# Exponentials on VectorE in an attention kernel: three SBUF passes for five, and groups that may open nearer to a unit's end

## The chip, the cores and the metric

The kernel runs on one core of one Trainium2 chip. The metric is the device time of one execution in microseconds (us). Each kernel was run in several rounds beside the kernel before on the same chip. One of the runs of the kernel before (993.6 us, in the series of e5 to e8) was slow and is not used. A ratio within 2% of 1 counts as "the same" in the record; where an interval below lies clear of 1, the difference is still called faster or slower here.

The engines are called as in the profile: PE is TensorE (matmul), ACT is ScalarE, DVE is VectorE, POOL is GpSimd, SP issues DMAs. In a profile, L1253 is a line of the kernel's source. The changed kernel is one to four lines shorter, so the same operation has a slightly lower line number there.

## The reference

One transformer block on 2,048 tokens of width 512: layer norm, attention with 32 heads of 16, residual, layer norm, a gated FFN of width 1,792, residual. What matters here is the softmax:

```python
scores = jnp.einsum("bhqd,bhkd->bhqk", q, k) * (Dh ** -0.5)   # 32 x 2048 x 2048
p = _softmax(scores, axis=-1)
o = jnp.einsum("bhqk,bhkd->bhqd", p, v)
```

That is 134 million exponentials. The kernel takes them as 2,048 tiles of 128 keys by 512 queries (for the last two query chunks: two key blocks by 256 queries).

## The kernel before

The program is not written down in its final order. A builder in Python holds streams of operations, each with an estimated duration, and emits them greedily: whatever can start first on an engine, by priority. Its order is then fixed, engine by engine. Work goes in 40 units (a query chunk and four heads): 24 of 64 tiles and 16 of 32.

Most tiles are exponentiated by ACT straight from PSUM, in steps of three and two tiles that use five PSUM banks in turn. A score step therefore waits for the exp two steps before it:

```python
SLOTS = ((0, 3), (3, 2))                       # PSUM banks of the two alternating steps
NRING = 15                                      # places of the ring PT that holds ACT's results
def exps():
    ...
    yield Op("act", 0.093 + 0.427 * n, ACTF(PT[:, p0:p0 + n, :], pbank[:, b0:b0 + n, :], ACT.Exp, scale=LN2 / 1024, bias=...))
```

An exp writes into PT, a ring of 15 tiles. It also has to wait until the PV matmul (the product with V) of the tile that was in its place before is done.

Some tiles go to DVE, in groups of up to four. A group takes four PSUM banks one after the other from the two that the dense work (projections, FFN) also uses. Each tile is converted to a 16-bit integer on its way from PSUM to SBUF, then the group is processed as a whole. The exponential comes out as a sum of two tiles, and PE sums them: it streams both against V.

```python
def dconv(G, j, b):                             # one per tile
    yield Op("dve", 0.7, ... tensor_scalar(out=dX[...], in0=pbank[:, b, :], scalar1=XMIN + 1024.0 * CENTER, scalar2=XMIN, op0=ALU.add, op1=ALU.max))
def dchain(G):                                  # once per group, five passes
    W = X & 0x3ff | 0x3c00                      # tensor_scalar
    W = W * W                                   # tensor_tensor
    W = -EK * ESCALE * W - ESCALE               # tensor_scalar
    E = (X >> 3) & 0x1f80                       # tensor_scalar
    X = W * X                                   # tensor_tensor
def pv():                                       # the group's part of it
    fns += prod(i, [dE2[:, d, j, :], dX[:, x, j, :].bitcast(BF16)])   # two PV streams per tile
```

(The passes are shortened here to what they compute.) Three rules decide when a group may open; there are three group buffers (`NX = 3`):

```python
GLAST = 32; DGAP = 6.0; DBUSY = 2.0; LOOK = 0.12; RATE = 1250
def room():        # no fourth group before the first one's PV; DVE not far behind; DGAP us since the last opening, ...
    ... C["gk"] - C["gpv"] >= NX ... sch.now >= C["dnext"] + (DBUSY if C["down"] < first_t[C["cdone"]] else 0)
def over(G):       # a group takes no more tiles once GLAST or fewer tiles of its unit are left
    return bool(G["t"]) and unit0[G["u"] + 1] - C["qpos"] <= GLAST
def pick(G):       # with fewer than GLAST + 12 tiles left, a new group is for the next unit
    u = unit_of(nxt) + (pos_of(nxt)[1] - pos_of(nxt)[0] < GLAST + 12)
```

Where PE would fall behind a rate of 1,250 columns per us the builder adds filler matmuls of zeros (`zero_bf` against `ones_bf`). At the end the kernel checks that all softmax sums lie in a range and runs a slower path if not.

## Time and profile before

The median of three runs was 913.09 us (912.94 to 913.13).

| what | view | before |
|---|---|---|
| PE, DVE, ACT busy | engine shares | 853.2, 738.0, 849.1 us of 909.8 |
| exp steps of ACT | groups by shape | 356 of three tiles, 356 of two: 1,780 tiles |
| tiles of DVE | conversions in the groups | 268, in 72 groups |
| ACT waiting for PE's attention matmuls | list of waits | 21.4 us, 36 waits |
| fillers | groups | 392, 133.7 us |

The page of the kernel before, engine shares:

```profile
PE 853.2 (94%) x7245; PEld 278.8 (31%) x7245; DVE 738.0 (81%) x1138; ACT 849.1 (93%) x782; POOL 210.6 (23%) x247
```

Its groups with shapes kept apart; after the count stand busy us, mean ns of one instruction, then the engine's idle time before them:

```profile
L1253 ACT ACTIVATE PT<-pbank 128x1536 bf16<-128x1536 f32 x356 | 533.3, 1498 | 21.4 <-PE pbank L1247 20.0
L1253 ACT ACTIVATE PT<-pbank 128x1024 bf16<-128x1024 f32 x356 | 383.5, 1077 | 1.5 <-PE pbank L1247 1.4
...
L1566 DVE TENSOR_SCALAR dX<-pbank 128x512 uint16<-128x512 f32 x268 | 181.5, 687 | 60.8 <-PE pbank L1247 58.7
L1582 DVE TENSOR_TENSOR dW<-dW 128x2048 f16<-128x2048 f16 x59 | 73.6, 1248 | 0.9
L1587 DVE TENSOR_TENSOR dX<-dW,dX 128x2048 bf16<-128x2048 bf16 x59 | 73.6, 1247 | 0.9
L1584 DVE TENSOR_SCALAR dE<-dX 128x2048 uint16<-128x2048 uint16 x59 | 44.7, 758 | 0.0
L1583 DVE TENSOR_SCALAR dW<-dW 128x2048 bf16<-128x2048 f16 x59 | 42.3, 717 | 0.7
...
L1581 DVE TENSOR_SCALAR dW<-dX 128x2048 uint16<-128x2048 uint16 x59 | 40.4, 685 | 0.4
```

ACT is the engine that is nearly always busy with the work that the softmax is made of. The two tensor_tensor passes of a full group take 1,248 and 1,247 ns, the tensor_scalar passes 685 to 758 ns.

The list of waits of ACT, its first line (us in total, times, longest):

```profile
ACT PT L1253 <- PE pbank L1247: 21.4, 36, 3.5
```

By the matmul whose semaphore came last before each exp in the trace, 17.1 us are for scores and 4.3 for PV.

Two stretches, one without FFN work and one with it (POOL is only used by the FFN there):

```profile
150.00:225.00 75.00, 67.77 (x525) 18.87 (x521) 69.08 (x96) 72.60 (x65) 0.00 (x0) 1.00 0.01 1
260.00:345.00 85.00, 80.78 (x553) 22.34 (x553) 71.12 (x98) 84.33 (x82) 48.45 (x40) 1.00 0.00 1
```

In the first, DVE is busy 69.1 of 75 us.

### The profile page before, as it was taken

To read this page: it belongs to the slowest core of one execution; us is meant where nothing else is said; L and a number is where in the kernel's file an instruction comes from. 1 tells how busy PE (TensorE), PEld (TensorE's weight loads), DVE (VectorE), ACT (ScalarE), POOL (GpSimd) and SP (SyncE) were. 2 spreads that over 40 slices of the span, in tenths; PEclk is the share of its full clock that TensorE was granted. 3 is DMA by queue.
4 is the path that set the end of the run, shared out by engine and by line. 5 is a ranking of instruction groups with operands and counts; after the bars stand their busy time and mean duration, and the time that the engine had idled before them with its cause. 6 is when DMAs were issued, how large, how long until landed. Compare 5 with 4: busy or idle time off the path is not lost.

```text
span 909.8 us, 17576 instructions
## 1 busy us (share of the span) xinstructions
PE 853.2 (94%) x7245; PEld 278.8 (31%) x7245; DVE 738.0 (81%) x1138; ACT 849.1 (93%) x782; POOL 210.6 (23%) x247
## 2 busy tenths in 40 slices
PE   8999999998999999999899999999999999999987
PEld 3322222222232222222232222222233333333435
DVE  7668899999888889799968888899977877876752
ACT  4699999999999999999999999999999999999951
POOL 5600000000034752000025743000004354340500
PEclk9999999999999999999999999999999999999999
DMA  5000061000000000000000000000000000001000
GB/s 186 1 1 1 1 223 34 1 1 2 12 1 1 1 2 1 18 18 2 1 12 1 2 1 7 13 18 1 1 14 13 2 1 1 2 7 30 1 13 16
DMA packets 12330, 15.11 MB, mean 17 GB/s; under 512 B 1744, under 2 KB 11216, under 8 KB 12240
## 3 DMA queue, kind: packets, MB, share of 16 engines
q1 hardware_dynamic: 12240, 13.90, 4.7%
q8 instruction: 58, 0.95, 0.4%
q14 instruction: 32, 0.26, 0.1%
HBM read 11.80 MB, written 2.10 MB: 15 GB/s over the span
## 4 chain that ended last, share of the span: by engine, by line
PE 50%; ACT 30%; issue 12%; DVE 6%; DMA 1%; SPq 0%; POOL 0%; ACTq 0%; DVEq 0%
ACT PT L1253 29%; PE pbank L1247 26%; PE pbank L1246 17%; PE pbank L1847 4%; PE pbank L1250 1%; ACT w_sb L1775 1%; DVE w_sb L1776 1%; DVE dX L1566 1%; DMA wqkv_sb<-in_A_wqkv_dram 1%; DVE OA L1653 1%; DVE dW L1582 1%; DVE dE L1584 0%; DVE QT L1391 0%; DVE g_sb L1765 0%; DVE dW L1581 0%
## 5 line engine op out<-in xcount | busy, mean ns | idle before, releaser
L1253 ACT ACTIVATE PT<-pbank 128x1536 bf16<-128x1536 f32 x712 | 819.5, 1288 | 22.9 <-PE pbank L1247 21.4
L1247 PE MATMUL pbank<-QT,KT 32*128 32x512 bf16 (+1 forms) x2560 | 313.0, 340 | 36.5 <-ACT PT L1253 28.9
L1566 DVE TENSOR_SCALAR dX<-pbank 128x512 uint16<-128x512 f32 x268 | 181.5, 687 | 60.8 <-PE pbank L1247 58.7
L1247 PE MATMUL pbank<-PT,VA 128*17 128x512 bf16 (+1 forms) x2235 | 180.0, 339 | 0.0
L1247 PEld LDWEIGHTS pbank<-QT,KT 32*128 32x128 bf16 x2560 | 82.8, 91 | 297.9 <-ACT PT L1253 207.6
L1847 PE MATMUL pbank<-ones_bf,zero_bf 128*128 128x512 bf16 x392 | 133.7, 386 | 6.4 <-DVE OA L1653 6.4
L1718 POOL TENSOR_SCALAR rstd<-mv 128x1 f32<-128x1 f32 x16 | 3.6, 226 | 483.2 <-DVE mv L1716 483.2
L1767 POOL TENSOR_TENSOR w_sb<-g_sb 128x512 f32<-128x512 f32 x49 | 65.1, 1330 | 167.8 <-DVE g_sb L1765 167.3
L1582 DVE TENSOR_TENSOR dW<-dW 128x2048 f16<-128x2048 f16 (+3 forms) x72 | 86.7, 1204 | 1.1
L1587 DVE TENSOR_TENSOR dX<-dW,dX 128x2048 bf16<-128x2048 bf16 (+3 forms) x72 | 85.2, 1184 | 1.1
L1247 PEld LDWEIGHTS pbank<-PT,VA 128*17 128x17 bf16 x2235 | 46.1, 87 | 107.4 <-issue 102.0
L1769 POOL TENSOR_TENSOR w_sb<-w_sb,g_sb 128x512 f32<-128x512 f32 x49 | 69.7, 1432 | 3.0
L1246 PE MATMUL pbank<-hnT_c,wg_sb 128*128 128x512 bf16 (+1 forms) x280 | 63.6, 339 | 1.0 <-ACT hnT_c L1692 0.5
L1246 PE MATMUL pbank<-hnT_c,wu_sb 128*128 128x512 bf16 (+1 forms) x280 | 62.8, 339 | 0.5 <-DVE dX L1566 0.4
L1246 PE MATMUL pbank<-wd_sb,GUT 128*128 128x512 bf16 x224 | 59.2, 382 | 0.0
L1584 DVE TENSOR_SCALAR dE<-dX 128x2048 uint16<-128x2048 uint16 (+3 forms) x72 | 52.6, 731 | 0.0
L1847 PEld LDWEIGHTS pbank<-ones_bf,zero_bf 128*128 128x128 bf16 x392 | 31.4, 96 | 68.3 <-issue 56.3
L1583 DVE TENSOR_SCALAR dW<-dW 128x2048 bf16<-128x2048 f16 (+3 forms) x72 | 50.1, 695 | 0.8
L1581 DVE TENSOR_SCALAR dW<-dX 128x2048 uint16<-128x2048 uint16 (+3 forms) x72 | 48.1, 668 | 0.4
L1776 DVE SCALAR_TENSOR_TENSOR w_sb<-w_sb,g_sb 128x512 f32<-128x512 f32 x49 | 40.6, 832 | 8.1 <-ACT w_sb L1775 7.7
L1799 DVE SCALAR_TENSOR_TENSOR GUT<-pbank,w_sb 128x512 bf16<-128x512 f32 x49 | 33.4, 687 | 14.8 <-PE pbank L1246 14.5
L1765 DVE COPY g_sb<-pbank 128x512 f32<-128x512 f32 x49 | 33.5, 685 | 10.7 <-PE pbank L1246 10.4
(89 smaller groups left out, 613.0 us busy)
## 6 DMA issues: line engine op xcount, KB each, us to landing
xres<-in_A_x_dram SPq DMA_DIRECT2D x16, 128.0 KB, 2.2
out_dram<-out_sb SPq DMA_DIRECT2D x16, 128.0 KB, 1.7
wg_sb<-in_B_w_gate_dram SPq DMA_DIRECT2D x1, 1792.0 KB, 7.1
wu_sb<-in_B_w_up_dram SPq DMA_DIRECT2D x1, 1792.0 KB, 11.9
wd_sb<-in_B_w_down_dram SPq DMA_DIRECT2D x1, 1792.0 KB, 17.3
x_sb<-in_A_x_dram SPq DMA_DIRECT2D x3, 512.0 KB, 8.6
wqkv_sb<-in_A_wqkv_dram SPq DMA_DIRECT2D x1, 896.0 KB, 7.7
x_sb<-in_A_x_dram SPq DMA_DIRECT2D x2, 256.0 KB, 2.9
```

The costliest lines, as they stand in the source:

```text
L1246: return lambda e: e.matmul(o, l, r, start=start, stop=stop)
L1247: return lambda e: e.matmul(o, l, r, start=start, stop=stop, tile_position=tile)
L1253: return lambda e: e.activation(out=o, in_=i, func=func, **kw)
L1566: yield Op("dve", 0.7, lambda e: e.tensor_scalar(out=dX[:, G["k"] % NX, j, :], in0=pbank[:, b, :], scalar1=XMIN + 1024.0 * CENTER, scalar2 ...
L1582: yield Op("dve", t2, lambda e: e.tensor_tensor(out=W, in0=W, in1=W, op=ALU.mult), reads=kW, writes=kW, port=True)
L1583: yield Op("dve", t1, lambda e: e.tensor_scalar(out=WB, in0=W, scalar1=-EK * ESCALE, scalar2=-ESCALE, op0=ALU.mult, op1=ALU.add), reads=kW ...
L1584: yield Op("dve", t1, lambda e: e.tensor_scalar(out=E.bitcast(U16), in0=X, scalar1=3, scalar2=0x1f80, op0=ALU.logical_shift_right, op1=ALU ...
L1587: yield Op("dve", t2, lambda e: e.tensor_tensor(out=X.bitcast(BF16), in0=WB, in1=X.bitcast(F16), op=ALU.mult), reads=kW + kX, writes=kX, p ...
L1767: yield Op("pool", 1.13, lambda e: e.tensor_tensor(out=ws, in0=gs, in1=gs, op=ALU.mult), reads=[("g", i)], writes=[("w", i)])
L1769: yield Op("pool", 1.3, lambda e: e.tensor_tensor(out=ws, in0=ws, in1=gs, op=ALU.mult), reads=[("w", i), ("g", i)], writes=[("w", i)])
L1776: yield Op("dve", 0.68, lambda e: e.scalar_tensor_tensor(out=ws, in0=ws, scalar=1.0, in1=gs, op0=ALU.add, op1=ALU.mult), reads=[("w", i), ...
L1847: fill_op = Op("pe", TMM, lambda e: e.matmul(pbank[:, PVB, :], zero_bf[:], ones_bf[:], start=False, stop=False, skip_group_check=True), re ...
```

## The change

The intent: with another split of the exponential, 2^n(1 + 2m/3 + m*m/3) up to a constant, three passes over a group are enough, and DVE's tiles stay fp16. DVE should then take more tiles from ACT. So that it can, a group takes tiles until 16 of the unit are left instead of 32 (the cut-off), a new one opens for a unit with at least 28 left instead of 44, and 3 us after the last instead of 6 (the gap).

```diff
-GLAST = 32
+GLAST = 16
-DGAP = 6.0
+DGAP = 3.0
-    dE2 = at("dE2", [128, NE, GS, 512], BF16)
+    dE2 = at("dE2", [128, NE, GS, 512], F16)
... (the exp's bias, the ones column of V, the V evacuation and the range check follow the new constants)
 def dchain(G):
-  ... tensor_scalar(out=W.bitcast(U16), in0=X, scalar1=0x3ff, scalar2=0x3c00, op0=ALU.bitwise_and, op1=ALU.bitwise_or)
-  ... tensor_tensor(out=W, in0=W, in1=W, op=ALU.mult)
-  ... tensor_scalar(out=WB, in0=W, scalar1=-EK * ESCALE, scalar2=-ESCALE, op0=ALU.mult, op1=ALU.add)
-  ... tensor_scalar(out=E.bitcast(U16), in0=X, scalar1=3, scalar2=0x1f80, op0=ALU.logical_shift_right, op1=ALU.bitwise_and)
+  ... tensor_scalar(out=W.bitcast(U16), in0=X, scalar1=0x3ff, scalar2=0xb800, op0=ALU.bitwise_and, op1=ALU.bitwise_or)
+  ... tensor_scalar(out=E.bitcast(U16), in0=X, scalar1=0x7c00, scalar2=0x8, op0=ALU.bitwise_and, op1=ALU.bitwise_or)
-  ... tensor_tensor(out=X.bitcast(BF16), in0=WB, in1=X.bitcast(F16), op=ALU.mult)
+  ... tensor_tensor(out=X.bitcast(F16), in0=W, in1=X.bitcast(F16), op=ALU.mult)
 def pv():
-  fns += prod(i, [dE2[:, d, j, :], dX[:, x, j, :].bitcast(BF16)])
+  fns += prod(i, [dE2[:, d, j, :], dX[:, x, j, :].bitcast(F16)])
```

More of the change, by code (lines that the diff above doesn't have):

```diff
@@ L1094 @@
 CENTER = 12
-EC, EK = 0.46167356, 0.16665046
-ESCALE = 2.0 ** -80
-VSCALE = 2.0 ** (95 - CENTER)
+EFIT = 1.5068958
+PSCALE = EFIT * 2.0 ** (CENTER - 15)
 def bass_sequential_preLN__mha_block__geglu_ffn__prompt_kernel(nc, A_x, A_wqkv, A_wo, B_x, B_w_gate, B_w_up, B_w_down, out):
@@ L1284, in consts @@
         yield Op("pool", 0.3, lambda e: e.tensor_copy(out=ident32[:], in_=ident[:]), reads=["ident"], writes=["ident32"])
-        yield Op("pool", 2.3, lambda e: e.memset(VA[:, :, :, 16:17], VSCALE), writes=["VA_ones"])
+        yield Op("pool", 2.3, lambda e: e.memset(VA[:, :, :, 16:17], 1.0), writes=["VA_ones"])
     def masks():
@@ L1402, in proj_v @@
                                       for dc in (2 * hf, 2 * hf + 1)], reads=rd, writes=[("pb", b)])
-            op = Op("dve", 0.61, lambda e, b=b, t=t: e.tensor_scalar(out=VA[:, t, :, 0:16], in0=pbank[:, b, :].rearrange("p (h i) -> p h i", i=16), scalar1=VSCALE, scalar2=None, op0=ALU.mult),
+            op = Op("dve", 0.61, lambda e, b=b, t=t: e.tensor_copy(out=VA[:, t, :, 0:16], in_=pbank[:, b, :].rearrange("p (h i) -> p h i", i=16)),
                     reads=[("pb", b)], writes=[("V", t)])
@@ L1490, in exps @@
             p0, n = an % NRING, len(mine)
-            yield Op("act", 0.093 + 0.427 * n, ACTF(PT[:, p0:p0 + n, :], pbank[:, b0:b0 + n, :], ACT.Exp, scale=LN2 / 1024, bias=-LN2 * (95 - CENTER) - math.log(EC)),
+            yield Op("act", 0.093 + 0.427 * n, ACTF(PT[:, p0:p0 + n, :], pbank[:, b0:b0 + n, :], ACT.Exp, scale=LN2 / 1024, bias=math.log(PSCALE)),
                      reads=[("pb", b0 + k) for k in range(n)], writes=[("PT", p0 + k) for k in range(n)],
@@ L1576, in dchain @@
         X, W, E = dX[:, x, 0:n, :], dW[:, 0:n, :], dE2[:, d, 0:n, :]
-        WB = W.bitcast(BF16)
         kX, kW, kE = [("dX", x, j) for j in range(n)], ["dW"], [("dE", d)]
@@ L1580, in dchain @@
         yield Wait(lambda: G["conv"] == n)
-        yield Op("dve", t1, lambda e: e.tensor_scalar(out=W.bitcast(U16), in0=X, scalar1=0x3ff, scalar2=0x3c00, op0=ALU.bitwise_and, op1=ALU.bitwise_or), reads=kX, writes=kW, port=True)
-        yield Op("dve", t2, lambda e: e.tensor_tensor(out=W, in0=W, in1=W, op=ALU.mult), reads=kW, writes=kW, port=True)
-        yield Op("dve", t1, lambda e: e.tensor_scalar(out=WB, in0=W, scalar1=-EK * ESCALE, scalar2=-ESCALE, op0=ALU.mult, op1=ALU.add), reads=kW, writes=kW, port=True)
-        yield Op("dve", t1, lambda e: e.tensor_scalar(out=E.bitcast(U16), in0=X, scalar1=3, scalar2=0x1f80, op0=ALU.logical_shift_right, op1=ALU.bitwise_and), reads=kX, writes=kE, port=True,
+        yield Op("dve", t1, lambda e: e.tensor_scalar(out=W.bitcast(U16), in0=X, scalar1=0x3ff, scalar2=0xb800, op0=ALU.bitwise_and, op1=ALU.bitwise_or), reads=kX, writes=kW, port=True)
+        yield Op("dve", t1, lambda e: e.tensor_scalar(out=E.bitcast(U16), in0=X, scalar1=0x7c00, scalar2=0x8, op0=ALU.bitwise_and, op1=ALU.bitwise_or), reads=kX, writes=kE, port=True,
                  gate=lambda: C["gpv"] >= G["k"] - NE + 1)
         C["gw"] += 1
-        yield Op("dve", t2, lambda e: e.tensor_tensor(out=X.bitcast(BF16), in0=WB, in1=X.bitcast(F16), op=ALU.mult), reads=kW + kX, writes=kX, port=True)
+        yield Op("dve", t2, lambda e: e.tensor_tensor(out=X.bitcast(F16), in0=W, in1=X.bitcast(F16), op=ALU.mult), reads=kW + kX, writes=kX, port=True)
         G["done"] = 1
@@ L1831, in check @@
         yield Op("dve", 0.1, lambda e: e.tensor_scalar(out=LCHK[:, n:n + 1], in0=probe[:, 0:1], scalar1=65535.0, scalar2=None, op0=ALU.is_equal), reads=["probe"] + [("LINV", u) for u in range(NU)], writes=["probe", "LCHK"])
-        yield Op("dve", 0.4, lambda e: e.tensor_scalar(out=LCHK[:, 0:n], in0=lf, scalar1=2.0 ** -40, scalar2=2.0 ** -10, op0=ALU.max, op1=ALU.min),
+        yield Op("dve", 0.4, lambda e: e.tensor_scalar(out=LCHK[:, 0:n], in0=lf, scalar1=2.0 ** -40, scalar2=2.0 ** -6, op0=ALU.max, op1=ALU.min),
                  reads=[("LINV", u) for u in range(NU)], writes=["LCHK"])
```

## The prediction

> **What bounds it now.** ScalarE. The table of engine shares gives ACT 849 of 909.8 us (93%). The group list gives its exps as 356 steps of three 512-column tiles at 1,498 ns and 356 of two at 1,077 ns: 0.515 us a tile. The list of waits gives ACT only 21.4 us of waiting for score matmuls. Exps run from 16 to 875 us; about 35 us of tail follow.
>
> Of 2,048 tiles, 268 go to VectorE, in 72 groups (59 are full). A full group costs it four conversions, about 2.5 us back to back (each recorded as 0.69, started 0.61 apart), and five passes: 0.69 + 1.25 + 0.72 + 0.76 + 1.25 = 4.66 us as recorded, about 4.5 back to back. Together 7.0 us. Where no FFN work runs (150 to 225 us) VectorE is busy 69.1 of 75 us and a group comes every 8 us: VectorE limits what it can take over. In FFN stretches (260 to 345 us) it takes only 12 to 14 tiles per 50 us against 26; VectorE is 84% busy there, TensorE 95%.
>
> **What the change removes, adds, moves.** Two passes go: the square (86.7 us in all) and the scale-and-offset (50.1 us). The three that stay keep shapes and widths, so durations should stay: about 0.69, 0.76, 1.25 us. The Trainium skill, "VectorE: DVE Perf Modes", section "What auto-detection actually checks", says that a two-tensor operation reaches only the two-per-cycle mode, a one-source one from SBUF four per cycle; the trace agrees (1.25 against 0.69 to 0.76 us): one expensive and one cheap pass go. A group then costs about 5.1 us, 27% less. The exp's bias, the ones column and the V evacuation cost the same. fp16 tiles against bf16 weights: no change expected, though no run here shows it yet.
>
> The smaller gap and the later cut-off let the freed time be used. Each tile moved saves ACT 0.515 us and costs TensorE about one more PV stream, an estimated 0.1 us; TensorE has 134 us of filler matmuls to give up, mostly outside FFN stretches.
>
> **How much is on the path.** Outside FFN work (about 375 us): tiles per 50 us go from 26 to 32 or 33 on top of ACT's 110, some 5%, 19 us. FFN stretches between 250 and 560 us: about 3.5%, 7 us. After 650 us, with small query chunks, few fillers and a nearly full TensorE: 1.5%, 3 us. Head and tail keep their length. Sum 29 us: 913 to 884 us. That is about 325 VectorE tiles in 85 to 90 groups, ACT exps near 888 us (summed durations) against 917, VectorE busy 690 us instead of 738, fillers down from 392 to about 300.
>
> **Chances.** 884 us, range 866 to 899. Faster by over 2% (under 894.8): 0.82; within 2%: 0.16; slower: 0.02.
>
> **What would show each step.** Three passes per group at unchanged durations; over 300 conversions; about 690 ACT exp steps instead of 712; groups every 6 us or less where no FFN runs. ACT should stay over 92% busy there; if its waits for score matmuls pass 45 us, TensorE or the PV order has become the limit.
>
> **What would make it wrong.** Groups limited by something other than VectorE time (two shared PSUM banks, three group buffers, the next unit's scores): tiles stay near 280, VectorE idles, time near 905. Late groups delaying a unit's last PV, so that ACT runs out of ring slots. TensorE filling up. On the other side, if VectorE stays 92% busy everywhere, 350 tiles and about 868 us. A failed range check would run the fallback and double the time.

## The result

The changed kernel takes 904.62 us (median of 4 runs, 901.49 to 905.76) beside 913.11 us before. Ratios are the mean time of one kernel's fast runs over that of the other's of the same rounds, so not quite the ratio of the medians: 0.9899, with a 95% interval of 0.988 to 0.9918. That is 1% faster, within the 2% that counts as the same. The range of 866 to 899 us does not hold it.

The same views of the changed kernel. Engine shares, groups by shape, the waits of ACT, the two stretches:

```profile
PE 852.3 (94%) x7220; PEld 277.2 (31%) x7220; DVE 682.1 (75%) x1093; ACT 827.7 (92%) x761; POOL 202.1 (22%) x247
```

```profile
L1252 ACT ACTIVATE PT<-pbank 128x1536 bf16<-128x1536 f32 x345 | 510.1, 1479 | 34.4 <-PE pbank L1246 32.8
L1252 ACT ACTIVATE PT<-pbank 128x1024 bf16<-128x1024 f32 x345 | 364.0, 1055 | 2.0 <-PE pbank L1246 1.8
...
L1565 DVE TENSOR_SCALAR dX<-pbank 128x512 uint16<-128x512 f32 x322 | 216.8, 686 | 86.4 <-PE pbank L1246 84.4
L1583 DVE TENSOR_TENSOR dX<-dW,dX 128x2048 f16<-128x2048 f16 x69 | 87.0, 1261 | 0.9
L1580 DVE TENSOR_SCALAR dE<-dX 128x2048 uint16<-128x2048 uint16 x69 | 51.7, 749 | 0.0
L1579 DVE TENSOR_SCALAR dW<-dX 128x2048 uint16<-128x2048 uint16 x69 | 50.7, 735 | 0.5
```

```profile
ACT PT L1252 <- PE pbank L1246: 34.6, 53, 3.5
```

```profile
150.00:225.00 75.00, 70.99 (x552) 19.87 (x551) 66.50 (x101) 74.13 (x66) 0.00 (x0) 1.00 0.01 1
260.00:345.00 85.00, 80.11 (x575) 22.04 (x574) 68.83 (x102) 83.67 (x80) 42.69 (x39) 1.00 0.00 1
```

Nearly everything that was forecast about the work is there: three passes at about their old durations (735 ns against 685 in the first, the others within 2%), 322 tiles (forecast 325) in 87 groups, 691 exp steps with the one odd one (690), DVE busy 682 us (690), 303 fillers (about 300). ACT is busy 21.4 us less (849.1 to 827.7). But the span fell by only 5.8 us in the profiled runs (909.8 to 904.0). So the time in which ACT does nothing grew from 60.7 to 76.3 us, by 15.6 us, and 13.2 us of that are waits for PE's attention matmuls (21.4 to 34.6): 10.3 us more for scores (17.1 to 27.4) and 2.9 us more for PV (4.3 to 7.2). The question is why ACT waits more.

The four runs differ by the granted clock: 901.49 us at 1.000, then 904.08 at 0.996, 905.16 at 0.994 and 905.76 us at 0.993. The trace's clock records show three stretches of 3.4 us at half speed in the profiled run and one that begins 2.7 us before its end; in the kernel before there is only one, 0.2 us before the end. By the four runs (905.76 less 901.49 us) that is worth some 4 us of the gap, not 20.

### The profile page after: what moved, and what is told of

It reads as the page before. It is cut to its first block, busy times and chain, and to the rows that moved or that the text cites. A ratio compares the mean times of both kernels' runs of the same rounds, so it can differ in the third digit from the quotient of the medians.

```text
span 904.0 us, 17467 instructions
## 1 busy us (share of the span) xinstructions
PE 852.3 (94%) x7220; PEld 277.2 (31%) x7220; DVE 682.1 (75%) x1093; ACT 827.7 (92%) x761; POOL 202.1 (22%) x247
## 4 chain that ended last, share of the span: by engine, by line
PE 57%; ACT 20%; DVE 11%; issue 10%; POOL 1%; ACTq 0%; DVEq 0%; POOLq 0%
PE pbank L1246 31%; ACT PT L1252 20%; PE pbank L1245 17%; PE pbank L1843 5%; DVE dX L1565 3%; PE pbank L1249 1%; DVE w_sb L1772 1%; DVE OA L1649 1%; DVE dE L1580 1%; PE pbank L1840 1%; DVE dX L1583 1%; DVE g_sb L1761 1%; ACT w_sb L1771 1%; DVE dW L1579 1%; PE pbank L1853 0%
## 5 line engine op out<-in xcount | busy, mean ns | idle before, releaser
L1252 ACT ACTIVATE PT<-pbank 128x1536 bf16<-128x1536 f32 (+1 forms) x691 | 796.7, 1266 | 36.5 <-PE pbank L1246 34.6
L1246 PE MATMUL pbank<-QT,KT 32*128 32x512 bf16 (+1 forms) x2560 | 320.6, 340 | 22.2 <-ACT PT L1252 17.0
L1565 DVE TENSOR_SCALAR dX<-pbank 128x512 uint16<-128x512 f32 x322 | 216.8, 686 | 86.4 <-PE pbank L1246 84.4
L1843 PE MATMUL pbank<-ones_bf,zero_bf 128*128 128x512 bf16 x303 | 105.4, 388 | 11.3 <-DVE OA L1649 11.3
L1583 DVE TENSOR_TENSOR dX<-dW,dX 128x2048 f16<-128x2048 f16 (+3 forms) x87 | 103.1, 1185 | 1.3
L1763 POOL TENSOR_TENSOR w_sb<-g_sb 128x512 f32<-128x512 f32 x49 | 55.7, 1137 | 163.0 <-DVE g_sb L1761 162.6
L1580 DVE TENSOR_SCALAR dE<-dX 128x2048 uint16<-128x2048 uint16 (+3 forms) x87 | 63.1, 725 | 0.0
L1579 DVE TENSOR_SCALAR dW<-dX 128x2048 uint16<-128x2048 uint16 (+3 forms) x87 | 60.6, 697 | 0.7
L1246 PE MATMUL pbank<-dE,VA 128*17 128x512 f16 (+1 forms) x385 | 38.0, 347 | 0.0
L1246 PE MATMUL pbank<-dX,VA 128*17 128x512 f16 (+1 forms) x385 | 37.6, 344 | 0.0
## 6 DMA issues: line engine op xcount, KB each, us to landing
wd_sb<-in_B_w_down_dram SPq DMA_DIRECT2D x1, 1792.0 KB, 16.6
```

The costliest lines, as they stand in the source:

```text
L1246: return lambda e: e.matmul(o, l, r, start=start, stop=stop, tile_position=tile)
L1252: return lambda e: e.activation(out=o, in_=i, func=func, **kw)
L1565: yield Op("dve", 0.7, lambda e: e.tensor_scalar(out=dX[:, G["k"] % NX, j, :], in0=pbank[:, b, :], scalar1=XMIN + 1024.0 * CENTER, scalar2 ...
L1579: yield Op("dve", t1, lambda e: e.tensor_scalar(out=W.bitcast(U16), in0=X, scalar1=0x3ff, scalar2=0xb800, op0=ALU.bitwise_and, op1=ALU.bit ...
L1580: yield Op("dve", t1, lambda e: e.tensor_scalar(out=E.bitcast(U16), in0=X, scalar1=0x7c00, scalar2=0x8, op0=ALU.bitwise_and, op1=ALU.bitwi ...
L1583: yield Op("dve", t2, lambda e: e.tensor_tensor(out=X.bitcast(F16), in0=W, in1=X.bitcast(F16), op=ALU.mult), reads=kW + kX, writes=kX, por ...
```

## The experiments

All kernels give the right result (e9 only by its slower path, see there). "Waits" are ACT's waits for scores and PV together, from the list of waits of the profiled run; "PV" is the part of them that a PV matmul ended, worked out from the trace's semaphores. "Tiles" are those of DVE. "Clock" is that of the profiled run.

| kernel | passes | cut-off | tiles | ACT busy, us | waits, us | PV, us | clock | median, us |
|---|---|---|---|---|---|---|---|---|
| before | 5 | 32 | 268 | 849.1 | 21.4 | 4.3 | 1.000 | 913.11 |
| after | 3 | 16 | 322 | 827.7 | 34.6 | 7.2 | 0.993 | 904.62 |
| e1 passes only | 3 | 32 | 293 | 840.1 | 44.1 | 17.1 | 0.992 | 923.34 |
| e2 passes and cut-off | 3 | 16 | 308 | 833.0 | 28.6 | 6.3 | 0.993 | 905.50 |
| e3 cut-off alone | 5 | 16 | 261 | 853.7 | 31.9 | 11.5 | 0.996 | 934.01 |
| e4 sum on DVE | 3+1 | 16 | 282 | 844.0 | 25.1 | 3.6 | 0.993 | 912.12 |
| e5 few fillers | 3 | 16 | 321 | 832.7 | 57.7 | 7.7 | 0.883 | 934.87 |
| e6 few fillers, before | 5 | 32 | 270 | 855.1 | 68.1 | 12.8 | 0.857 | 969.74 |
| e7 more fillers | 3 | 16 | 325 | 834.0 | 77.3 | 38.8 | 0.998 | 955.33 |
| e8 cut-off 18 | 3 | 18 | 308 | 832.9 | 29.9 | 11.7 | 0.998 | 907.81 |
| e9 look-ahead 0.10, before | 5 | 32 | 268 | | 41.6 | 16.6 | | (fallback) |
| e10 look-ahead 0.10, after | 3 | 16 | 324 | 827.0 | 38.8 | 12.5 | 0.995 | 908.51 |
| e11 PV sets apart | 3 | 32 | 284 | 842.0 | 25.1 | 4.4 | 0.998 | 911.39 |
| e12 other constants | 3 | 16 | 326 | 824.4 | 23.4 | 2.9 | 0.997 | 890.56 |
| e13 new numbers, old order | 5 | 32 | 268 | 849.3 | 23.8 | 5.7 | 0.995 | 913.06 |
| e14 look-ahead 0.14, before | 5 | 32 | 265 | 853.1 | 37.0 | 7.4 | 0.984 | 929.56 |
| e15 look-ahead 0.14, after | 3 | 16 | 322 | 826.8 | 36.9 | 6.8 | 0.987 | 912.26 |
| e16 constants of e12, before | 5 | 32 | 262 | 854.2 | 32.7 | 12.3 | 0.996 | 934.49 |

ACT's busy time follows the tiles within some 3 us, but for e5 to e7, where it is 5 to 10 us higher than in kernels with about as many tiles (a likely reason: exps overlap in the records only where ACT does not wait, and these three wait most). The waits do not follow the tiles, and they are what moves the time about.

### e1, e2, e3: the parts of the change

```diff
e1  -GLAST = 16    +GLAST = 32      -DGAP = 3.0   +DGAP = 6.0      (from the changed kernel)
e2  -DGAP = 3.0    +DGAP = 6.0                                     (from the changed kernel)
e3  -GLAST = 32    +GLAST = 16                                     (from the kernel before)
```

> Three passes, with the old gap (6) and the old cut-off (32); its program moves 293 tiles to VectorE instead of 268 (after: 322). Theory T1 (TensorE is what the moved tiles run into: each costs it nearly what ScalarE saves): the gain is small and roughly in step with the tiles, so 906 to 911 us. Rival T2 (the later cut-off hurts: groups that open late hold up the last PV of a unit and eat a larger gain of the passes): this is at least as fast as the whole change, 904 us or less, with fewer waits of TensorE for VectorE.

> Three passes and the new cut-off (16), old gap (6): 308 tiles. T1: between e1 and the whole change, 903 to 908 us. T2: as slow as the whole change or slower, while e1 is faster. If the gap is what hurts, this is clearly faster than the whole change (under 900).

> The kernel before, five passes, with only the cut-off at 16; the smaller gap makes no difference to that program. 261 tiles, seven fewer than before. T1: the same as before or up to 5 us slower (910 to 918). T2: clearly slower than before (over 920), since the slower chains hold up the units' ends more.

Measured: e1 923.34 us, ratio 1.0101 (1.0082 to 1.0121). The three passes alone, with 25 more tiles, are slower than the kernel before. Neither theory had that. e2 is at 905.50, so the gap of 3 us is worth under 1 us: it brings 14 tiles (308 to 322) and 6.0 us more waits (28.6 to 34.6), which about cancel. e3 is at 934.01, ratio 1.0225. T2 expected e3 but not e1. The parts do not add: plus 10, plus 21, and together minus 8.5.

e1 also answers a reading of the prediction. This is the stretch without FFN work in e1:

```profile
150.00:225.00 75.00, 66.24 (x510) 19.41 (x517) 48.70 (x72) 72.25 (x64) 0.00 (x0) 1.00 0.00 1
```

DVE fell from 69.1 to 48.7 us of 75. The conversions in the same stretch (busy us, count) of before, e1, e2, e3 and the changed kernel:

```profile
150.00:225.00 75.00, 24.92 (x38) 1.00 0.01 1
150.00:225.00 75.00, 24.70 (x38) 1.00 0.00 1
150.00:225.00 75.00, 28.98 (x44) 1.00 0.01 1
150.00:225.00 75.00, 24.14 (x36) 1.00 0.00 1
150.00:225.00 75.00, 34.71 (x53) 1.00 0.01 1
```

e1 converted 38 tiles, exactly as many as before. So a faster DVE alone takes no more tiles in this stretch: with the old rules each unit there has three groups of four, before and in e1. The later cut-off alone brings no more either while the passes are five (e3: 36). With three passes it brings 44 (e2), and the smaller gap 53. It takes the shorter passes and the rules together.

What made e1 slower is visible at a unit's start. PE in e1, in order of time (start, us):

```profile
166.86 0.39 PE L1246 MATMUL pbank<-dE,VA 128*17 128x512 f16 x4
167.08 0.39 PE L1246 MATMUL pbank<-dX,VA 128*17 128x512 f16 x4
167.40 0.40 PE L1246 MATMUL pbank<-QT,KT 32*128 32x512 bf16 x4
167.73 0.39 PE L1246 MATMUL pbank<-dE,VA 128*17 128x512 f16 x4
167.95 0.39 PE L1246 MATMUL pbank<-dX,VA 128*17 128x512 f16 x4
168.27 0.39 PE L1246 MATMUL pbank<-QT,KT 32*128 32x512 bf16 x2
168.59 0.39 PE L1246 MATMUL pbank<-dE,VA 128*17 128x512 f16 x4
168.81 0.39 PE L1246 MATMUL pbank<-dX,VA 128*17 128x512 f16 x4
169.13 0.39 PE L1246 MATMUL pbank<-QT,KT 32*128 32x512 bf16 x1
169.44 0.61 PE L1246 MATMUL pbank<-PT,VA 128*17 128x512 bf16 x8
```

and ACT in the same stretch:

```profile
164.36 3.54 ACT L1252 ACTIVATE PT<-pbank 128x1024 bf16<-128x1024 f32 x3
169.89 3.71 ACT L1252 ACTIVATE PT<-pbank 128x1536 bf16<-128x1536 f32 x3 [1.99 <-PE pbank L1246]
```

and one conversion of DVE:

```profile
169.55 0.69 DVE L1565 TENSOR_SCALAR dX<-pbank 128x512 uint16<-128x512 f32 x1 [0.98 <-PE pbank L1246]
```

All three groups of the unit have long been ready (the last chain ends at 160.7), and their double PV sets (dE and dX) come within 2.3 us. Behind them, at 169.44, stand the PV matmuls of ACT's own tiles, and ACT waits 1.99 us for the first four of these. It does not wait for scores: those of its step are three of the four at 167.40 and end at 167.79; the two at 168.27 are the next step's, and the one at 169.13 is DVE's tile, converted at 169.55. The first four PV matmuls end at 169.84, and the exp starts at 169.89: it had no free place in PT. The prediction had named ring slots as a risk, but from groups that come late; these come early and together. In the kernel before, three sets of a comparable unit (its sixth) come 2.5, 3.6 and 11.9 us after the unit's start; in e1, 3.1, 3.9 and 4.8 us. The Trainium skill ("TensorE: Matmul & The Clock Gate", section "The mechanism") says that matmuls start and end strictly in program order; the trace agrees here, since the PV matmuls at 169.44 start only after the three double sets and the scores, although ACT waits for them. The lines also show that a lone score matmul holds PE for 0.31 us (169.13 to 169.44) and a set of four for 0.33 us (167.40 to 167.73).

### e11: is it the bunch?

```diff
-if "done" in G and "pv" not in G and m and (m == nm - 1 or sch.done[...] <= sch.now + 0.1):
+if "done" in G and "pv" not in G and m and (m == nm - 1 or sch.now >= C.get("dlast", 0.0) + 4.0) and (m == nm - 1 or sch.done[...] <= sch.now + 0.1):
+                        C["dlast"] = sch.now                       (from e1; after G["pv"] = 1)
```

> e1 (three passes, old cut-off and gap, 923 us) with one rule added: the PV matmuls of two groups stand at least 4 us apart, except at a unit's end; 284 tiles, nine fewer than e1. Theory T7 (with the old cut-off and faster chains all three groups of a unit are ready at its start, and their PV sets, 0.54 us each, come in a bunch in front of the scores): ScalarE's waits fall from 44 us to under 30 and the time to 908 to 914 us. If the bunch is not what hurts: nine tiles fewer, so 923 to 928 us.

Measured: 911.39 us, waits 25.1 us. The waits of e1 and of e11:

```profile
ACT PT L1252 <- PE pbank L1246: 44.1, 61, 3.5
ACT PT L1252 <- PE pbank L1246: 25.1, 40, 3.5
```

Nine tiles fewer, yet 12 us faster than e1, as T7 forecast, because ACT waits 19 us less. In e1's trace 26 of 79 groups' PV sets start less than 2 us after the one before, in e11's one of 78. Counted from the traces, waits that have two or more set starts between 3 us before them and their end fall from 13.2 us (all for PV) to 1.3. So the bunch accounts for some 12 of the 19 us, through PV and the ring; the rest fell elsewhere in the new order. The changed kernel has only 1.0 us of such waits, so the bunch does not explain its own 13.2 us. e11 also shows that the three passes with the old rules, even so spread, are worth nothing against the kernel before (ratio 0.999, 0.9964 to 1.0015).

### e4: one PV stream per tile

```diff
+        yield Op("dve", t2, lambda e: e.tensor_tensor(out=X.bitcast(F16), in0=E, in1=X.bitcast(F16), op=ALU.add), ...)   # end of dchain
-fns += prod(i, [dE2[:, d, j, :], dX[:, x, j, :].bitcast(F16)])
+fns += prod(i, [dX[:, x, j, :].bitcast(F16)])
-Op("pe", 2 * TPV + 0.1 * (r - 1), cols=256 * len(G["t"]), ...)
+Op("pe", TPV + 0.05 * (r - 1), cols=128 * len(G["t"]), ...)
```

> The whole change plus one VectorE pass per group that adds the two products, so that TensorE streams one PV set per group and not two: a group costs VectorE about 1.25 us more and TensorE about 0.27 us less; 282 tiles in 77 groups. T1: fewer tiles, but ScalarE waits less for score matmuls (under 25 us against 34.6), and the time is no worse than 906 us in spite of 40 fewer tiles. T2 or any theory in which VectorE is in the way: slower than the whole change by what 40 tiles are worth on ScalarE, 18 us, so about 920 us.

Measured: 912.12 us, waits 25.1 us. Both sides miss. The waits did fall by 9.5 us, at the edge of what T1 asked for, but the 40 lost tiles cost ACT 16.3 us of busy time (844.0 against 827.7). Whether the waits fell through PE's smaller load or through another order, this run cannot tell: e9 and e14 below move them by more with the order alone. Moving the sum back to DVE does not pay.

### e5, e6, e7: fillers and the clock

```diff
e5, e6  -RATE = 1250   +RATE = 600       (e5 from the changed kernel, e6 from the kernel before)
e7      -RATE = 1250   +RATE = 1500      (from the changed kernel)
```

> The whole change with the filler rate at 600 columns per us in place of 1,250, which leaves about 30 of 324 fillers; 321 tiles, so ScalarE has the same work. Theory T1 (TensorE is crowded: fillers and the moved tiles' matmuls stand in front of the scores that ScalarE waits for): ScalarE's waits for score matmuls fall from 34.6 us to 25 or less and the time to 890 to 898 us. Theory T3 (the order is a matter of luck, TensorE's load plays no part): 900 to 908 us. Theory T4 (the clock is what costs): fewer fillers lower the granted clock further, under 0.97, and the time rises over 906 us.

> The kernel before with the same low filler rate; 268 tiles or nearly. T1: it has only 21 us of waits to lose, and TensorE has more room, so it gains less than the changed kernel does: 906 to 913 us. If it gains as much as e5 does or more, the fillers cost both kernels alike and do not explain why the change gained so little. T4: slower than 914 us, with a lower clock.

> The whole change with the filler rate at 1,500; about 640 fillers in place of 324, 325 tiles. T1: ScalarE's waits for score matmuls at least double, over 65 us, and the time is 930 to 945 us. T4 (the clock): the clock is 1.000 in every run and the time is 902 us or less. T3: within 8 us of the whole change.

Measured: e5 934.87, e6 969.74, e7 955.33 us. e7 bears T1 out and overshoots its range: with twice the fillers (597 and 30 others, against 303 and 21) and a clock of 0.998, the waits rise from 34.6 to 77.3 us, 31.6 us of it for PV. What stands in PE's queue does cost ACT. e5 (ratio 1.0249, 1.0175 to 1.0324, on both sides of the 2%) does not test T1, because the clock fell, as T4 expected. The granted clock of e5, and of the kernel before with few fillers (e6), in tenths over 40 slices:

```profile
PEclk9999988567898999977799999986676799899999
```

```profile
PEclk9999976575898999956598898976599987899989
```

So the fillers cannot simply be taken out: they hold the clock. With few of them the changed kernel loses 30 us and the kernel before 57. The changed kernel is then 35 us faster, which is a hint that the change is worth more than 9 us, but no more than a hint, as the clocks differ too (0.883 and 0.857).

### e8: a slightly different cut-off

```diff
-GLAST = 16   +GLAST = 18
```

> The whole change with the cut-off at 18 in place of 16: 308 tiles, 14 fewer, worth 6 us of ScalarE at 0.43 us a tile. T3 (the time hangs on the particular order that the builder happens to find): 912 us or more, as ScalarE's idle time rises by over 5 us although TensorE has less to do for moved tiles. T1 alone: TensorE has slightly less to do, so idle time is no larger, and the time is at most 6 us more than the whole change, 905 to 910 us.

Measured: 907.81 us, waits 29.9. This is what T1 allows, and not the scatter that T3 asked for.

### e9, e10, e14, e15: another order of the same work

The builder's look-ahead says how much later than the earliest candidate an operation of higher priority may start and still be taken. It changes no instruction, only which comes first; the group openings then differ a little.

```diff
e9, e10   -LOOK = 0.12   +LOOK = 0.10     (e9, e14 from the kernel before;
e14, e15  -LOOK = 0.12   +LOOK = 0.14      e10, e15 from the changed kernel)
```

> The kernel before with nothing changed but the builder's look-ahead, 0.10 in place of 0.12: another order of the same instructions, 268 tiles in 74 groups, the same five passes and constants. Theory T3 (ScalarE's idle time belongs to the particular order, and the kernel before has an unusually good one): 925 to 935 us, with ScalarE's waits for score matmuls over 30 us against 21. Theory T1 (idle time follows TensorE's load): the same work, so within 4 us of before, 909 to 917 us.

> The whole change with the look-ahead at 0.10: 324 tiles in 85 groups. T3: it has no tuned order to lose, so about as fast as the whole change, 900 to 910 us, and 20 us or more (over 2%) faster than e9, its partner at the same look-ahead. T1: the same distance from e9 as the whole change from before, about 9 us.

> The kernel before with the look-ahead at 0.14: another order, 265 tiles. T3 (the kernel before has an unusually good order): 920 to 930 us and ScalarE's waits for score matmuls over 28 us. T1 (idle time follows TensorE's load): within 4 us of before.

> The whole change with the look-ahead at 0.14: 322 tiles in 83 groups. T3: its own scatter, 902 to 915 us, and 12 us or more below e14. T1: 904 us, 9 us below before.

e9 took 2,408.79 us: the kernel's own range check failed, so the slower path ran after the fast one and gave the right result. Why it failed is not known. Its time is no measurement, but its trace holds the fast path. ACT's waits in it, and the last addition to an output, beside that of the kernel before and of e10:

```profile
ACT PT L1253 <- PE pbank L1247: 41.6, 60, 4.3
```

```profile
928.50 0.69 DVE L1817 TENSOR_TENSOR out_sb<-pbank,h_c 128x512 bf16<-128x512 f32 x1 [2.33 <-PE pbank L1246]
```

```profile
904.63 0.69 DVE L1817 TENSOR_TENSOR out_sb<-pbank,h_c 128x512 bf16<-128x512 f32 x1 [2.33 <-PE pbank L1246]
```

```profile
902.31 0.69 DVE L1813 TENSOR_TENSOR out_sb<-pbank,h_c 128x512 bf16<-128x512 f32 x1 [2.33 <-PE pbank L1245]
```

With the same 268 tiles, five passes and constants, the last output comes 23.9 us later (928.50 against 904.63) and ACT waits 20.2 us more. e14 repeats it with nearly the same work (265 tiles): 929.56 us, ratio 1.0165 (1.0132 to 1.0198), with a right result from the fast path. Its waits:

```profile
ACT PT L1253 <- PE pbank L1247: 37.0, 46, 3.4
```

Part of this is clock: e9 has 13.7 us at half speed before its last output and e14 27.3 us, the kernel before none. At like clocks e14 is still 12 us slower (926.44 us at 0.994 beside 914.53 at 0.995). T1, which allowed 4 us for the same work, falls. The changed kernel moves far less under the same settings: 908.51 and 912.26 us. At 0.14 the change is worth 17.3 us (at the same clock of 0.986, 931.76 less 913.70, 18.1 us), at 0.10 about 26 us by the last output (928.50 to 902.31), and at the setting that both kernels came with 8.5 us.

### e13: the new arithmetic in the old order

```diff
-GLAST = 16   +GLAST = 32      -DGAP = 3.0   +DGAP = 6.0
+        yield Op("dve", t1, ... (out=W, in0=X, 0x3ff, 0x3c00, bitwise_and, bitwise_or))      # two passes whose result is overwritten
+        yield Op("dve", t2, ... (out=W, in0=W, in1=W, op=ALU.mult))
```

> The new arithmetic (fp16 tiles, new constants) with two idle VectorE passes of the old sizes, and the old gap and cut-off: the builder finds the very order of the kernel before, 268 tiles, five passes. If the new arithmetic costs or saves nothing by itself: 911 to 915 us, the same as before. If fp16 tiles beside bf16 weights slow TensorE, or the added dummy passes clash: over 918 us.

Measured: 913.06 us, ratio 0.9991 (0.9972 to 1.0011), 17,576 instructions as before, and these waits:

```profile
ACT PT L1252 <- PE pbank L1246: 23.8, 37, 3.5
```

fp16 tiles against bf16 weights and the new constants cost nothing that shows. What the change does to the time comes from the two dropped passes and from what is done when.

### e12, e16: a third order, for both kernels

```diff
e12  -DGAP = 3.0  +DGAP = 4.0    -DBUSY = 2.0  +DBUSY = 1.0    -DFROM = 20  +DFROM = 24     (from the changed kernel)
e16  -DGAP = 6.0  +DGAP = 4.0    -DBUSY = 2.0  +DBUSY = 1.0    -DFROM = 20  +DFROM = 24     (from the kernel before)
```

> The whole change with three other constants of the builder (gap 4, extra gap under FFN backlog 1 in place of 2, groups from projection 24 in place of 20), picked as the shortest of 250 plans: 326 tiles in 88 groups. T3: a better order gives back part of what was lost; ScalarE's waits under 30 us and 893 to 900 us. T1: TensorE has slightly more to do, so no faster than the whole change, 902 to 908 us.

> The kernel before with the three other constants of e12 (gap 4, extra gap 1, start 24), five passes, cut-off 32. If those constants are good in themselves: 900 us or less, and e12 owes its gain to them and not to the passes. T3: they only pick another order, and here a worse one: 925 to 940 us.

`DBUSY` is added to the gap while FFN output of finished query chunks is outstanding, and before `DFROM` operations of the projections are done no group opens. All three constants only choose when groups open. They were picked as the shortest plan, by the builder's own estimate, of some 250; that estimate served for the choice alone.

Measured: e12 890.56 us, ratio 0.9758 (0.9727 to 0.9788), a little under what T3 gave; e16 934.49 us, ratio 1.0237. The constants are not good in themselves: they pick an order, a good one for the three-pass kernel and a poor one for the other. e12 beats both kernels. The record has no such search for the five-pass kernel, so how much a new search alone would give it is open. Engine shares and ACT's waits of e12:

```profile
PE 842.4 (95%) x7230; PEld 275.3 (31%) x7230; DVE 689.4 (78%) x1100; ACT 824.4 (93%) x759; POOL 206.1 (23%) x247
```

```profile
ACT PT L1252 <- PE pbank L1246: 23.4, 34, 3.5
```

With 326 tiles the waits are back at 23.4 us, near the kernel before, and most of the tile term arrives. e12 gives PE as much work as the changed kernel does (four tiles more, 7,230 matmuls against 7,220, 323 fillers against 324), so that work alone does not bring the waits. ACT's busy time is 24.7 us lower than before (824.4 against 849.1) and the span is 20.6 us lower (889.2 against 909.8). The clock of 0.997 and a waits term of 2.0 us more are part of the rest.

## Why the prediction was wrong

**What held.** The passes and their durations: 1,261, 749 and 735 ns for a full group, against about 1.25, 0.76 and 0.69 us forecast. The number of tiles and groups, ACT's steps, DVE's busy time and the fillers came within a few per cent. That the changed arithmetic costs nothing elsewhere was right (e13). ACT's waits stayed below the 45 us that the prediction set as an alarm; the alarm was set too high.

**The step that failed** is "How much is on the path ... Sum 29 us". It turned the moved tiles into time as if the rest of the schedule stayed as it was: the prediction took ACT's idle time from the old trace and kept it. In its place the runs showed two terms of similar size:

- Tiles: minus 21.4 us of ACT's busy time in the profiled run.
- Idle time of ACT: plus 15.6 us, 13.2 of them waits for scores (10.3) and PV (2.9).

The difference is the 5.8 us by which the span fell.

Why did the idle time grow? What the runs show is that it goes with the order: the order alone moves it by as much (e9, e14), and the added work without a bad order does not bring it (e12). The kernel before has an order with unusually little of it: 21.4 us of waits, and 23.8 us where the same order was kept with the new arithmetic (e13). The four other orders of the five-pass kernel at the same filler rate (e3, e9, e14, e16) have 31.9 to 41.6 us. The changed kernel's 34.6 us is an ordinary value. A change that touches when groups open cannot keep the old order, and 15.6 of the 21.4 us of the tile term went into idle time. That the kernel before had a good order, and the changed one an ordinary one, is luck as far as the prediction goes: nothing in it looked at this. At two settings for which neither kernel had been tuned the change is worth 17.3 us (0.14) and some 26 us (0.10, from traces), and e12 found a good order for the three-pass kernel, 22.4 us below before. These settings are a small sample, and e12 was chosen as the best of many plans; they show the size of the scatter, not its distribution.

**The mis-sized tile term.** 0.515 us per tile came from adding recorded durations. Consecutive exps overlap in the records: in the trace of before, where one follows another without a gap, they start 1.330 us after a step of three and 0.903 us after a step of two, which is 0.447 us per tile (2.233 over 5), with records that overlap by 0.14 us in the median. The Trainium skill ("ScalarE: Activation LUTs", section "What ACT_TABLE_LOAD costs") says that back-to-back ACTIVATEs overlap by about 93 ns; the trace has more, but it was there to be read. 54 tiles at 0.447 us are 24.1 us, an estimate from the trace; the page has 21.4.

**DVE as the limit.** "VectorE limits what it can take over" outside FFN stretches was wrong as a reading: in e1 DVE became faster, fell to 48.7 us busy of 75, and took the same 38 tiles. A high busy share of an engine whose work is admitted by a rule does not show that its speed is the limit. The forecast of tiles came out right because the change also moved the rules; the rule alone would not have done (e3: 36 tiles there, 261 in all), so five passes were a limit right behind it.

**PE's price per moved tile.** The estimate was 0.1 us. PE without its fillers was busy 713.9 us before (853.2 less 133.7 and 5.6) and 739.6 us after (852.3 less 105.4 and 7.3): 25.7 us for 54 tiles, 0.48 us each, part of it at half clock; in e12 it is 16.3 us for 58 tiles, 0.28 us each. Besides the second PV stream, a lone score matmul costs nearly as much as a set of four (0.31 against 0.33 us above), and so does a PV set that lost a tile (323 ns for three, 326 for four, medians between starts in the trace of before). This puts more into PE's queue, which by e7 can cost ACT time, though in e12 it did not. How the 13.2 us divide between this load, the order and the half-speed stretches is not settled.

**The gap.** It did next to nothing for the time (e2: 905.50 against 904.62 us), as its 14 tiles came with 6.0 us more waits.

**What stays open.** Which property makes an order good. One is shown for e1, PV sets that do not stand together (e11); in the changed kernel such bunches make 1.0 us of its waits. What makes the rest of these was not separated by any experiment. And why e9 failed its range check.

## What to carry to other kernels

When a program's order is found by a greedy builder, compare families and not single builds: shift a constant that adds no work, on both sides, and see how far the time moves before giving a difference of 1 or 2% to a change. After a change of durations, search the builder's constants again; here that gave 14 us more than the change as it came. Where a list of waits names only a line and a tile, look in the order of time which instruction ended the wait: here two kinds of waits stood in one line. And before calling an engine the limit of what it may take, find the rule that admits its work, and check that it would take more if it were faster.

## What the Trainium skill lacked or had wrong

- "TensorE: Matmul & The Clock Gate", Part 1: it gives a free-running window of about 3.4 us and the states of half and full clock. The traces' clock records agree: half-speed stretches of 3.4 us or multiples of it. Its rule against PE-idle gaps of over about 3.4 us (section "HAM oscillation — how this bites in real kernels") does not cover e5 by itself: e5 had a mean clock of 0.883 with PE busy 91% of the span and no gap above 2.75 us between matmuls. The page's next section ("A second HAM failure mode: psum-queue depth-cycling") does tell of short idle gaps that make the clock oscillate, but gives no number for how much idling is too much.
- "ScalarE: Activation LUTs": overlap of back-to-back ACTIVATEs of about 93 ns; here 143 ns in the kernel before (medians of 327 pairs after 1,536 columns and of 277 after 1,024).
- The same page gives the overlap, but no page that was read says how far a sum of recorded durations can be off a throughput: here 0.515 us per tile by sum, 0.447 by start to start.
- No page that was read speaks of fp16 moving tiles against bf16 weights: e13 shows no cost (ratio 0.9991).
